# A retention and gated-MLP kernel: the planner's arrival time of program packets, and another order of loads and work

## The chip, the cores and the metric

The kernel runs on one core of a Trainium2 chip. The metric is the device time of one execution in microseconds, the median of the runs. It was 203.94 us before the change, over three runs from 202.18 to 205.26 us.

## The reference

Inputs are q, k, v of shape (4 batches, 8 heads, 768 tokens, 64), all float32, and the MLP's weights. A retention layer feeds a gated MLP:

```
state[b,h] = gamma[h] * state[b,h] + outer(k[t], v[t])
y[b,h,t]   = q[t] @ state[b,h] / 8
x    = y as (batch, 768, 512)
gate = sigmoid(causal depthwise convolution of x with conv_w, 5 taps)
out  = (gate * (x @ w_val)) @ w_out          # both weights 512 x 512
```

The output is (4, 768, 512) in float32.

## The kernel before

**Tiling.** The 768 tokens are cut into 6 chunks of 128, and a chunk of one batch is a "group" g (24 groups, chunk by chunk, the 4 batches within). Retention is done in chunks: scores of q and k, a mask, scores times v, and the state of earlier chunks times q. For the first four groups (chunk 0, batches 0 to 3) the steps stand apart: `first_scores` (called s below, L446 to L455), `first_mask` on VectorE, `first_y` (y, L523 to L532), `evac` (VectorE multiplies y by decay rows into the tile x, L588), `round_x` (ScalarE's cast xh) and `rest_x` (GpSimd's xl), and `first_state` (z, both halves of the state). The decay rows come from `first_pos` (p, a product of two matmuls with two rows each, L568) that `base_copy` moves out of PSUM. From group 4 on one `visit` (v) does the whole group in 128 small matmuls of 64x64, in two bursts. A `head` (h) opens them.

**The MLP.** x @ w_val is split in three products of rounded parts to keep float32 accuracy: `val_tile` (V, L1061; its matmuls in `val`, L719) has 12 matmuls of 512 columns per tile of 128 channels, 4 tiles per chunk. It ends in a gate (convolution on ScalarE and VectorE, a sigmoid) and a multiplication. The second product (O) is `out_tile` with 12 matmuls of 512 columns for chunks 0 and 5, and for chunks 1 to 4 seven block products of 12 matmuls of 256 columns. Weights arrive as 64-bit values and are converted on chip by ScalarE, VectorE and GpSimd (`convert`, w).

**Loads.** All input goes through SyncE's queue. The first 14 loads stand in `LOADS` (L61 to L64): ("a", g) is q, k and v of group g (768 KB), ("q", 0) is q and k of group 0 (512 KB), ("v", 0) its v (256 KB), ("k", g) the second layout of k that the state needs (256 KB), ("w", n) a weight row block (512 KB), and ("t", 0) the small table of decay and mask factors (68 KB). Later loads follow when a buffer is free.

**The order.** `WORK` (L66 to L70) is a string with one letter per PE step in the order of their due times. `plan` (L105 on) turns it into the instruction order of all engines on the host, ahead of time: a list scheduler that takes the step with the smallest rank among those ready, with a table of costs. The steps depend on each other by the tiles that they read and write. Where PE would wait early on, the planner puts filler matmuls on zeros into the order (L271 to L285); they are real instructions, and what follows them on PE follows in order.

**Program packets.** PE's program arrives by DMA in packets of 16 KB. The planner counts pairs (one weight load and one matmul): the first request is made after 71 pairs, each later one after 127.6 (L41). `fetch` sets when the packet that was asked for is usable. It looks at the loads that are in the list `sent` at that moment: the packet begins after the loads issued before the request, within limits, and is usable a little later. `offered` holds large loads back after 26 us of plan time, until PE is a set time past its last request.

In the planner of before, the time is worked out at the request, so a load that the planner takes up afterwards, though it starts earlier, is not in the list:

```
queued = max((x for t, x in sent if t <= asked + AHEAD), default=0.0)
later = min(max(asked + LEAD, queued + BEHIND), asked + WORST + 0.4 * (asked < 12.0)) + USABLE
```

Of the kernel before, what the change touches and what calls it, by code (L numbers as in the profile page):

```python
# [39 lines left out]
COLD, WARM_AT = 1.85, 5.0  # L40
FIRST_PAGE, PAGE = 71, 127.6  # L41
LEAD, AHEAD, BEHIND, WORST, USABLE, DEPTH = 1.0, 0.2, -0.9, 4.5, 2.4, 23
HOLD_FROM, HOLD, HOLD_LAG = 26.0, 30, 1.1
FIRST_BYTE, PER_MB = 2.85, 2.65
LATE_MB, LATE = 3.0, 1.2
TABLES = (4.6, 4.6)
# [12 lines left out]
FILLED_VALS = 24  # L59
CONV_LEAD, CHUNK = 7.0, 2.4  # L60
LOADS = (  # L61
    ("q", 0), ("t", 0), ("a", 1), ("v", 0), ("a", 2), ("w", 0), ("k", 1), ("a", 3),
    ("w", 1), ("w", 2), ("k", 0), ("w", 3), ("k", 2), ("k", 3),
)  # L64

WORK = (  # L66
    "spsysyzysyVzwzVwwhVzvVwvOOvOvOTvVvVvVVOvVOVv"
    "OVvvOvVOOOvVOOOOVVvOvVvVOVOVVOOOvvOOOvOvOOVO"
    "OOVOVVOOOOO"
)  # L70

# [33 lines left out]
def plan(steps, filler, last, into):  # L105
# [46 lines left out]
    left = [0] * len(steps)  # L152
# [8 lines left out]
    while ends:  # L161
        t = ends.pop()
# [8 lines left out]
    clock, free = {}, {}  # L171
# [8 lines left out]
        if not s.waits:  # L180
            offer(s)
    order, landed, moved = [], 0.0, 0.0
    left, need, usable, later = float(FIRST_PAGE), float(FIRST_PAGE + DEPTH), 0.0, 0.0
    kind, sent, asked_at = "big", [], -1e9

    def fetch(now):

        nonlocal left, need, usable, later, asked_at  # L190
        if left <= 1e-9:
            asked = max(now, usable)
            asked_at = asked
            queued = max((x for t, x in sent if t <= asked + AHEAD), default=0.0)
            later = min(max(asked + LEAD, queued + BEHIND), asked + WORST + 0.4 * (asked < 12.0)) + USABLE
            left = PAGE
        else:
            now = max(now, usable)
            usable, need = later, PAGE
        return now  # L200

    def run_pe(s, now):
        nonlocal left, need, kind
        slow = COLD if now < WARM_AT else 1.0
        if s.small:
            if kind == "big":
                now += INTO
            kind = "small"
            todo, each = s.small, PAIR * s.wide * slow
        else:  # L210
            if kind == "small":
                now += OUT_OF
            kind = "big"
            todo, each = s.big, s.gap / max(1, s.big) * slow
        while todo > min(left, need):
            x = min(left, need)
            now += x * each
            todo -= x
            left -= x
            need -= x  # L220
            now = fetch(now)
        left -= todo
        need -= todo
        now += todo * each
        return now, now + (0.21 if s.small else 0.17) * slow
# [9 lines left out]

    def offered(e):
        if e == "DMA" and patient and max(clock[e], clock["PE"]) > HOLD_FROM:
            if left <= HOLD or clock["PE"] < asked_at + HOLD_LAG:
                return [s for s in free[e] if s.mb < 0.4]
        return free[e] if e != "PE" or held is None else [s for s in free[e] if s is held]  # L240

# [18 lines left out]
    while any(free.values()):  # L260
        patient = True
        patient = any(offered(e) for e in free)
        start, _, e = min(
            (round(max(clock[e], min(max(s.ready, s.own if s.engine == e else 0.0) for s in offered(e))), 6), e, e)
            for e in free
            if offered(e)
        )
        s = min(
# [3 lines left out]
        if e == "PE":  # L272
# [5 lines left out]
            for i in range(int((start - since) * FILLED / FILL) if filling else 0):  # L278
# [4 lines left out]
                x = min(left, 2.0 if ring == into[0] else 4.0)  # L283
# [34 lines left out]
        if s.turn:  # L318

            t, e = s.turn, s.turn.engine  # L320
# [10 lines left out]
def tile_retention_gated_mlp(  # L331
# [930 lines left out]
    with tc.manual_schedule():  # L1262
        for step in plan(steps, filler, vals[FILLED_VALS], ("ye", "sc")):
            traced = nc.cur_bb.bb.instructions
            seen = len(traced)
            step.fn(*step.args)
            if step.engine == "PE":
                traced_as[step] = [i.name for i in traced[seen:] if i.engine == mybir.EngineType.PE]
            if step.behind:


                first, at = step.behind
                names = traced_as[first]
                tc.add_manual_dep(
                    traced[-1], names[min(int(at / PAIR) // 2 if first.small else 0, len(names) - 1)],
                    mybir.DependencyInfo(mybir.DependencyClass.Sync, mybir.DependencyReason.DATA), reason="load",
                )
# [93 lines left out]
```

## Time and profile before

| what | value |
|---|---|
| runs | 202.18, 203.94, 205.26 us |
| profiled execution | 205.48 us, its span 203.7 us |
| PE (matmul) busy | 196.7 us, 97% of the span |
| PEld (weight loads) | 168.5 us, 83% |
| VectorE / ScalarE / GpSimd | 130.3 / 110.2 / 140.4 us |
| DMA | 36.28 MB, mean 178 GB/s |
| chain that ended last | PE 86%, DMA 7%, VectorE 2% |

The profiled execution is 1.54 us above the median of the runs, and its span leaves 1.8 us outside. Matmuls are pipelined, so the ends of the records overlap the next ones; the starts tell more than the busy sum. In the rows below the times are microseconds from the span's start, and in brackets stands what ended an idle time.

### The profile page before, as it was taken

The numbers are of one execution on the slowest core, as the hardware profiler recorded it, in microseconds if no ns is written. First come the engines' busy times: TensorE is split into PE (matmuls) and PEld (weight loads), VectorE is DVE, ScalarE is ACT, GpSimd is POOL, SyncE is SP. The second block draws the span as 40 slices with busy tenths as digits, with TensorE's granted clock in tenths as the row PEclk, the third lists the DMA queues.
The fourth block names the chain that finished last, engine by engine and source line by source line (L and its number), as shares of the span: only waits on it lengthen the run. The fifth ranks groups of instructions, "written<-read, shape, count | busy, mean of one in ns | idle before, by whom it ended". The sixth has DMA issues, their size and how long they took to land.

```text
span 203.7 us, 8356 instructions
## 1 busy us (share of the span) xinstructions
PE 196.7 (97%) x3732; PEld 168.5 (83%) x3732; DVE 130.3 (64%) x200; ACT 110.2 (54%) x225; POOL 140.4 (69%) x120
## 2 busy tenths in 40 slices
PE   8899999999997999999999999999999999999993
PEld 5579876888885879899889899888889989888883
DVE  1355799862239986998489995998412558993100
ACT  3558867975177656965376566244433336612221
POOL 0049976899699986999949994766993799122500
PEclk9979999999999999999999999999999999999999
DMA  6999895578675640197657377311100122122022
GB/s 215 388 418 372 272 407 230 216 254 286 195 292 215 227 193 6 29 363 287 211 206 253 118 262 259 154 53 55 53 2 0 55 94 67 51 77 80 1 103 103
DMA packets 11303, 36.28 MB, mean 178 GB/s; under 512 B 1154, under 2 KB 5634, under 8 KB 8708
## 3 DMA queue, kind: packets, MB, share of 16 engines
q1 hardware_dynamic: 5472, 29.43, 39.2%
q10 hardware_dynamic: 5796, 6.32, 9.0%
q8 instruction: 29, 0.48, 0.9%
q14 instruction: 6, 0.05, 0.1%
HBM read 29.46 MB, written 6.29 MB: 176 GB/s over the span
## 4 chain that ended last, share of the span: by engine, by line
PE 86%; DMA 7%; DVE 2%; ACT 1%; issue 1%; SPq 0%; ACTq 0%
PE mm L726 33%; PE mm L803 20%; PE sy L511 10%; PE mm L846 8%; PE z_ps L495 5%; PE sy L433 4%; DMA out_dram<-o_sb 4%; DMA att<-in_att_dram 3%; PE sy L886 3%; PE ye L528 1%; DVE acc L710 1%; PE z_ps L451 1%; PE sy L451 1%; DVE u L483 0%; ACT o_sb L859 0%
## 5 line engine op out<-in xcount | busy, mean ns | idle before, releaser
L710 DVE SCALAR_TENSOR_TENSOR acc<-x,cw_sb,acc 128x512 f32<-128x512 f32 x96 | 68.2, 748 | 7.7 <-ACT acc L708 7.4
L606 POOL TENSOR_TENSOR xl<-x,xh 128x512 fp32r<-128x512 f32 x24 | 30.9, 1288 | 17.3 <-ACT xh L601 15.6
L788 POOL TENSOR_TENSOR gvl<-gate,gvh 128x512 fp32r<-128x512 f32 x24 | 30.9, 1296 | 9.2 <-ACT gvh L784 7.3
L726 PE MATMUL mm<-xl,wvh 128*128 128x512 f32 x96 | 31.0, 398 | 0.0
L726 PE MATMUL mm<-xh,wvh 128*128 128x512 f32 x96 | 30.9, 404 | 0.0
L422 POOL TENSOR_TENSOR att<-att,small_sb 128x512 f32<-128x512 f32 x24 | 25.1, 1046 | 7.6 <-DMA att<-in_att_dram 4.2
L726 PE MATMUL mm<-xh,wvl 128*128 128x512 f32 x96 | 27.7, 396 | 0.0
L741 DVE TENSOR_TENSOR gate<-mm,gate 128x512 f32<-128x512 f32 x24 | 16.5, 687 | 13.8 <-PE mm L726 12.7
L460 DVE TENSOR_TENSOR u<-sy,small_sb 128x512 f32<-128x512 f32 x20 | 13.7, 684 | 14.2 <-PE sy L433 14.2
L784 ACT CAST gvh<-gate 128x512 fp32r<-128x512 f32 x24 | 14.4, 618 | 15.1 <-DVE gate L741 11.9
L771 POOL TENSOR_TENSOR gate<-gate 128x512 f32<-128x512 f32 x16 | 20.7, 1297 | 1.8 <-DVE gate L741 1.5
L506 ACT COPY snap<-z_ps 128x256 f32<-128x256 f32 x40 | 13.8, 375 | 14.2 <-PE z_ps L495 13.1
L726 PEld LDWEIGHTS mm<-xh,wvl 128*128 128x128 f32 x96 | 17.9, 188 | 4.0
L726 PEld LDWEIGHTS mm<-xl,wvh 128*128 128x128 f32 x96 | 17.9, 188 | 3.9
L601 ACT CAST xh<-x 128x512 fp32r<-128x512 f32 x24 | 14.8, 617 | 10.6 <-DVE x L591 10.6
L718 ACT ACTIVATE gate<-acc 128x512 f32<-128x512 f32 x24 | 14.3, 600 | 11.5 <-DVE acc L710 6.0
L708 ACT ACTIVATE acc<-x,cw_sb 128x512 f32<-128x512 f32 x24 | 16.5, 692 | 7.4 <-DVE x L591 6.5
L752 POOL TENSOR_TENSOR gvl<-gate,gvh 128x512 fp32r<-128x512 f32 x8 | 10.3, 1289 | 14.4 <-ACT gvh L748 14.3
L726 PEld LDWEIGHTS mm<-xh,wvh 128*128 128x128 f32 x96 | 17.1, 188 | 3.3
L591 DVE TENSOR_TENSOR x<-sy,dec 128x512 f32<-128x512 f32 x20 | 13.6, 681 | 5.4 <-PE sy L433 4.6
L511 PEld LDWEIGHTS sy<-u,att 64*64 64x64 f32 x640 | 11.2, 134 | 6.6 <-issue 2.2
L511 PE MATMUL sy<-u,att 64*64 64x64 f32 x640 | 13.9, 224 | 1.5 <-DVE x L591 1.5
(79 smaller groups left out, 380.5 us busy)
## 6 DMA issues: line engine op xcount, KB each, us to landing
att<-in_att_dram SPq DMA_DIRECT2D x20, 1024.0 KB, 6.9
wst<-in_w_dram SPq DMA_DIRECT2D x8, 512.0 KB, 9.4
out_dram<-o_sb ACTq DMA_DIRECT2D x15, 256.0 KB, 3.2
att<-in_att_dram SPq DMA_DIRECT2D x3, 768.0 KB, 8.7
out_dram<-top ACTq DMA_DIRECT2D x8, 256.0 KB, 3.8
att<-in_att_dram SPq DMA_DIRECT2D x5, 256.0 KB, 8.7
att<-in_att_dram SPq DMA_DIRECT2D x1, 512.0 KB, 3.7
out_dram<-gate ACTq DMA_DIRECT2D x2, 128.0 KB, 1.7
```

Of the source, the lines that this page charges most:

```text
L422: nc.gpsimd.tensor_tensor(v, v, vd_sb[:, c, :].unsqueeze(2).broadcast_to([P, 8, HALF]), op=ALU.mult)
L511: nc.tensor.matmul(sy[cols, h, off:off + HALF], lhsT=lhsT, rhs=rhs, start=start, stop=True, skip_group_check=True,)
L601: nc.scalar.copy(xh[n][:, :, b], xs[n][:, :, b, HALO:])
L606: nc.gpsimd.tensor_tensor(xl[n][:, :, b], xs[n][:, :, b, HALO:], xh[n][:, :, b].bitcast(F32), op=ALU.subtract)
L708: nc.scalar.mul(acc, x[:, :, 0:P], cw_sb[:, m, 0:1])
L710: nc.vector.scalar_tensor_tensor(acc, x[:, :, k:k + P], cw_sb[:, m, k:k + 1], acc, op0=ALU.mult, op1=ALU.add,)
L726: nc.tensor.matmul(vps[n, m], lhsT=w[:, m, ct * P:(ct + 1) * P], rhs=xx[n][:, ct].rearrange("p b t -> p (b t)"), start=(i == 0), stop=(i = ...
L741: nc.vector.tensor_tensor(gv, vps.pop((n, m)), gv, op=ALU.mult)
L771: engine.tensor_tensor(block(n, k), block(n, a), block(n, b), op=getattr(ALU, op))
L788: engine.tensor_tensor(low, block(n, k), operands[n, k, 0].bitcast(F32), op=ALU.subtract)
L803: nc.tensor.matmul(banks[bank][:, tt * 256:(tt + 1) * 256], lhsT=g[:, ct, tt * P:(tt + 1) * P], rhs=weight(w, part % 2)[:, ct], start=(k i ...
L846: nc.tensor.matmul(ops[n, b, cs.start][:, 0:cs.stop - cs.start], lhsT=gg[:, b * P:(b + 1) * P], rhs=w[:, ct, cs], start=(i == 0), stop=(i ...
```

## The change

Three edits. The planner works out a packet's arrival at the next request, from all loads issued up to the request, with a fixed time for requests before 12 us of plan time, and a cap of 4.2 in place of 4.5 between 12 and 26 us. `LOADS` and `WORK` get another order: v of group 0 goes up to second place ahead of the table, group 3 goes ahead of all second layouts of k, and of those group 1's is last. In `WORK` p is the first letter, s comes earlier, z stands twice ahead of the first V, and four V and one O stand ahead of the first visit. The upper limit on the hold of large loads is 99 and larger than any distance between requests.

```diff
-HOLD_FROM, HOLD, HOLD_LAG = 26.0, 30, 1.1
+HOLD_FROM, HOLD, HOLD_LAG, HOLD_WINDOW = 26.0, 30, 1.1, 99.0
 LOADS = (
-    ("q", 0), ("t", 0), ("a", 1), ("v", 0), ("a", 2), ("w", 0), ("k", 1), ("a", 3),
-    ("w", 1), ("w", 2), ("k", 0), ("w", 3), ("k", 2), ("k", 3),
+    ("q", 0), ("v", 0), ("t", 0), ("a", 1), ("a", 2), ("w", 0), ("a", 3), ("w", 1),
+    ("k", 0), ("w", 2), ("w", 3), ("k", 3), ("k", 2), ("k", 1),
 )
 WORK = (
-    "spsysyzysyVzwzVwwhVzvVwvOOvOvOTvVvVvVVOvVOVv"
-    "OVvvOvVOOOvVOOOOVVvOvVvVOVOVVOOOvvOOOvOvOOVO"
+    "psyssyzsyyzwwVzwVhwzVVOvvvOOvOvVvVvVvVOVTvVO"
+    "vOVOvOVOOvOVOvvVOOOOVvOvVVOVOvOVVOOvvOOOvOVO"
     "OOVOVVOOOOO"
 )
+    def arrival():
+        if asked_at < 12.0:
+            return asked_at + 5.0 + USABLE
+        began = asked_at + LEAD
+        if asked_at < HOLD_FROM:
+            queued = max((x for t, x in sent if t <= asked_at + AHEAD), default=0.0)
+            return min(max(began, queued + BEHIND), asked_at + 4.2) + USABLE
+        for t, x in sorted(sent):
+            if t <= asked_at + AHEAD:
+                began = max(began, x + BEHIND)
+        return min(began, asked_at + WORST) + USABLE
     def fetch(now):
         if left <= 1e-9:
-            asked = max(now, usable)
-            asked_at = asked
-            queued = max((x for t, x in sent if t <= asked + AHEAD), default=0.0)
-            later = min(max(asked + LEAD, queued + BEHIND), asked + WORST + 0.4 * (asked < 12.0)) + USABLE
+            if asked_at > -1e8:
+                usable = arrival()
+            asked_at = max(now, usable)
             left = PAGE
         else:
             now = max(now, usable)
-            usable, need = later, PAGE
+            need = PAGE
     def offered(e):
-            if left <= HOLD or clock["PE"] < asked_at + HOLD_LAG:
+            if left <= HOLD or not 0 <= clock["PE"] - asked_at - HOLD_LAG <= HOLD_WINDOW:
```

## Rows read from the trace of the kernel before

**Rows 1.** Stages: stretch, length; busy us (instructions) by engine; clock, DMA share, GB/s
```profile
22.90:61.90 39.00, 39.00 (x866) 31.07 (x859) 24.68 (x38) 26.68 (x57) 32.76 (x29) 1.00 0.75 269
61.90:63.43 1.53, 0.02 (x1) 0.00 (x0) 1.53 (x4) 1.00 (x4) 1.53 (x2) 1.00 0.91 344
63.43:189.28 125.85, 125.71 (x2374) 111.46 (x2375) 94.16 (x144) 65.98 (x132) 94.70 (x79) 1.00 0.37 130
```

**Rows 2.** Waits of PE: who waited for whom; us in total, times, longest
```profile
PE sy L511 <- DVE x L591: 1.5, 1, 1.5
...
PE ye L879 <- PEq L1358: 0.8, 1, 0.8
```

**Rows 3.** Chain of waits, 48 to 64 us: start, us, what
```profile
48.80 8.18 DMA out_dram<-o_sb
...
57.06 0.18 ACT o_sb L859
...
62.78 0.61 DVE x L591
```

**Rows 4.** Timeline of PE, 5 to 23 us: start, us, engine, line, operation
```profile
5.46 1.26 PE L451 MATMUL sy<-att 64*64 64x128 f32 x32
...
6.65 1.12 PE L570 MATMUL ye<-u 2*128 2x512 f32 x2
...
8.73 0.90 PE L451 MATMUL z_ps<-att 64*64 64x128 f32 x32 [0.96 <-DMA att<-in_att_dram]
...
11.95 1.42 PE L451 MATMUL sy<-att 64*64 64x128 f32 x32
...
15.93 1.60 PE L886 MATMUL sy<-const-float32-0.0 128*128 128x128 f32 x12
...
17.47 0.90 PE L451 MATMUL z_ps<-att 64*64 64x128 f32 x32
...
20.28 1.60 PE L886 MATMUL sy<-const-float32-0.0 128*128 128x128 f32 x12
...
21.81 1.16 PE L495 MATMUL z_ps<-att 64*64 64x64 f32 x64
...
22.90 1.20 PE L726 MATMUL mm<-xh,wvh 128*128 128x512 f32 x4
```

**Rows 5.** Timeline of VectorE, ScalarE and GpSimd in the start
```profile
4.62 0.76 DVE L472 TENSOR_TENSOR xh<-small_sb 128x256 f32<-128x256 f32 x2 [3.69 <-DMA small_sb<-in_small_dram]
...
18.43 0.96 DVE L483 TENSOR_TENSOR u<-z_ps,xh 128x768 f32<-128x768 f32 x1 [1.67 <-PE z_ps L451]
...
19.43 1.05 POOL L422 TENSOR_TENSOR att<-att,small_sb 128x512 f32<-128x512 f32 x1
...
20.41 0.69 DVE L591 TENSOR_TENSOR x<-ye,base 128x512 f32<-128x512 f32 x1 [0.43 <-PE ye L528]
...
21.14 0.62 ACT L601 CAST xh<-x 128x512 fp32r<-128x512 f32 x1 [0.50 <-DVE x L591]
```

**Rows 6.** DMA issues at 2.5, 4.4 and 12.5 us; last column us to landing
```profile
att<-in_att_dram SPq DMA_DIRECT2D x1, 768.0 KB, 8.7
...
att<-in_att_dram SPq DMA_DIRECT2D x1, 768.0 KB, 10.7
...
att<-in_att_dram SPq DMA_DIRECT2D x1, 256.0 KB, 8.4
```

**Rows 7.** Stage with the reduced clock, columns as in Rows 1
```profile
9.80:13.00 3.20, 3.20 (x57) 2.86 (x55) 1.54 (x2) 2.06 (x6) 0.58 (x1) 0.50 1.04 423
```

**Rows 8.** Pairs up to two requests; DMA queues in 91.9:93 and 158.2:159.3
```profile
0.00:88.07 88.07, 84.40 (x1985) 68.87 (x1989) 57.51 (x89) 58.71 (x126) 66.03 (x60) 0.98 0.68 251
...
0.00:157.43 157.43, 153.76 (x3261) 130.43 (x3265) 107.78 (x166) 94.11 (x196) 121.37 (x105) 0.99 0.58 210
...
q8 instruction: 1, 0.02, 5.0%
...
q8 instruction: 1, 0.02, 7.7%
```

More of the change, by code (lines that the diff above doesn't have):

```diff
@@ L182, in plan @@
     order, landed, moved = [], 0.0, 0.0
-    left, need, usable, later = float(FIRST_PAGE), float(FIRST_PAGE + DEPTH), 0.0, 0.0
+    left, need, usable = float(FIRST_PAGE), float(FIRST_PAGE + DEPTH), 0.0
     kind, sent, asked_at = "big", [], -1e9
+    def arrival():
[9 more added lines that the diff above has]
+        return min(began, asked_at + WORST) + USABLE
     def fetch(now):
-        nonlocal left, need, usable, later, asked_at
+        nonlocal left, need, usable, asked_at
         if left <= 1e-9:
-            asked = max(now, usable)
-            asked_at = asked
-            queued = max((x for t, x in sent if t <= asked + AHEAD), default=0.0)
-            later = min(max(asked + LEAD, queued + BEHIND), asked + WORST + 0.4 * (asked < 12.0)) + USABLE
+            if asked_at > -1e8:
+                usable = arrival()
+            asked_at = max(now, usable)
             left = PAGE
```

## The prediction

> **What bounds the kernel now.** I read the stages first, then PE's waits, then the chain of waits where it leaves PE, then the timeline of the start. From 22.90 us, where the first V begins, PE's busy time fills its stages: 39.00 of 39.00 us, then 125.71 of 125.85 us. Between them lies one hole of 1.53 us [rows 1]. The list of PE's waits shows the same hole as a wait for an evacuation by VectorE, and besides it a wait of 0.8 us for PE's own sequencer at the very start [rows 2]. So after 22.90 us the time is the sum of PE's work, the hole and a tail, and the number of matmuls there does not change with the order. What an order can change is when V begins, what PE has already done by then, and the holes.
>
> The hole has its origin in a store: one output transfer issued at 48.80 us took 8.18 us, ScalarE's next copy into that buffer could only go on at 57.06 us, VectorE's taps came late behind it, and the evacuation for which PE waited began at 62.78 us [rows 3].
>
> The start is a chain through group 3. Its load was issued at about 4.4 us and landed 10.7 us later, at 15.1 us [rows 6]. Yet its scores began at 17.47 us: PE first did 12 filler matmuls, 15.93 us on, 1.60 us long [rows 4]. The planner had put them there to cover a wait that was over by then. After the scores come the mask at 18.43, the evacuation at 20.41 and the cast at 21.14, which ends at 21.76 us [rows 5]. PE fills 20.28 us on with another 12 fillers, and only at 21.81 us does it do the first two z, 64 small matmuls in 1.09 us up to V's start [rows 4].
>
> **The change part by part.**
>
> *Loads.* In the old list 3.82 MB end with group 3's load (0.5, 0.07, 0.75, 0.25, 0.75, 0.5, 0.25, 0.75 in its order), in the new one 3.57. Group 2's load, issued at 2.5 us, lands at 11.2 us, group 3's 1.5 MB of queue later at 15.1 us [rows 6], which is 2.6 us per MB. The 0.25 MB less are worth 0.65 us: group 3 lands at about 14.5 us. Group 1's load and the table come 0.25 MB later, 0.65 us. Group 1's scores now start at 8.73 us after an idle 0.96 us [rows 4], so they go to 9.4 us; group 2's load keeps its place, and the next scores after those start at 11.95 us [rows 4], so 1.5 us of slack take it. The mask factors, at 4.62 us and 0.76 us long [rows 5], go to about 6.0 us at their end; the first mask needs them after the scores at 5.46 us have ended, 6.7 us now and later with p in front. That costs nothing, and without this cover 0.65 us.
>
> *p first.* It takes 1.12 us and now comes after the first scores, which start at 5.46 us and take 1.26 us [rows 4]. With p first they start at 6.6 and end at 7.8 us. What hides it is the idle stretch up to 8.73 us and the later load of group 1; if that cover goes, it costs 1.12 us.
>
> *s before y, and z ahead of V.* The new string lets group 3's scores go ahead of the third y, since tile dependencies follow the string. The scores can begin at 14.5 us at best. At worst PE comes to them as late behind the load as now (17.47 less 15.1, 2.4 us), at 16.9 us. I take 15.4 us, nearer to the best: PE is one y ahead of where it was, and the second half of the fillers (0.8 us) may still stand there. From the scores' start to the end of the cast it is now 4.29 us [rows 4, 5]. In the new order VectorE does one more evacuation in this chain, 0.69 us [rows 5], ahead of the last y; most of it, 0.6 us, is added: 4.9 us. So V can begin at 20.3 us in place of 22.90, a gross 2.6 us. Of the two z that lie ahead of V now, the first can slip into the chain's gaps, where PE does 1.60 us of fillers now: its k moves up from 5.07 to 4.32 MB, and GpSimd's scaling takes 1.05 us [rows 5]. The second needs group 1's k, now last in the list. The last load lands at 12.5 + 8.4 = 20.9 us [rows 6] and, the bytes being the same, does so again; with 1.05 us of scaling it is 22 us. So this z follows inside the V's and is 0.55 us that PE no longer has behind it. Net 2.05 us. With 14.5 us it is 2.95 us, with 16.9 us 0.55 us. If group 3's scores stay at 17.47 us, the longer chain (0.6) and the covered z (0.55) cancel: zero, the lower bound. A loss from this part would need V's own weights to be late; w 0 keeps its 2.82 MB, and w 1 moves up by 0.25 MB.
>
> *The clock.* From 9.80 to 13.00 us PE was granted 0.50, its level of 1.2 GHz, after the idle 0.96 us and the scores at 8.73; the scores at 11.95 took 1.42 us there, those at 17.47, at full clock, 0.90 us [rows 4, 7]. If such a stretch falls on scores, y and z after 14.5 us, each loses some 0.5 us, three of them 1.5 us. In the sum I leave the clock as it is; this bound lies inside the range of the term above (2.05 less 1.5 is 0.55).
>
> *The planner's packets.* The code computes no time on the chip; it only moves loads and fillers. No wait for a packet stands among PE's waits after the first [rows 2], so there is no such stall to remove: zero, and the nearest price for one that is made is the 0.8 us of that wait. That packets do wait for loads the trace shows twice. The planner's request falls on pair 1985 at 88.07 us, in a stretch with large loads, and the packet moved in 91.9 to 93 us, 3.8 us or more later; the one at pair 3261, 157.43 us, with only stores about, moved after 158.2 us, within 1.9 us [rows 8]. The Trainium skill, "DMA: Bandwidth & Descriptors", section "Queues, rings and completion order", says that each DMA engine goes round robin between the queue rows that have work, a packet at a time. By that rule a program packet would not stand behind loads issued earlier, the new waits would be plan fiction, and the sum would hold nothing for the planner's edit but misplaced fillers, as in the first rival. The two requests speak against it.
>
> *The later order.* Four V and one O stand ahead of the first visit, and visits come in other places. PE's work is the same: zero, as long as VectorE, ScalarE and GpSimd deliver. In the stage after 63.43 us they are busy for 94.16, 65.98 and 94.70 of 125.85 us [rows 1]. The last 11 letters are the same, so the tail is too. The hole of 1.53 us comes from a store among loads, and the new order puts the first stores elsewhere; it may go. Late next would be the evacuation that the following visit waits for.
>
> **The sum.** The profiled execution took 205.48 us. Less 2.05 us for the start and 1.53 us for the hole it is 201.9 us. It lies 1.54 us above the median of 203.94 us, just the hole's size, so I take it that the median run had none of it: 203.94 less 2.05 is 201.9 us as well.
>
> **The rivals.** *First, the start gains nothing:* fillers again stand in front of group 3's scores, because the planner's idea of the landing is wrong in the new order too. For it speaks that the fillers of 15.93 us were such an error; against it that the scores are now ahead of y and the packet's wait is set anew. The time stays at 203.9 us. *Second, all goes:* the scores start with the landing, 2.95 us, and the hole is a part of the median run as well and disappears. Then it is 203.94 − 2.95 − 1.53 = 199.5 us. Against it speaks that the fastest run before, 202.18 us, can hardly have had the hole, and then the median need not. *Third, slower:* the visits are bunched, and each waits for the evacuation of the one before. One such wait costs 1.5 us [rows 2]. It is in the stretch of "Ovvv" behind the first O and of the next "vv": with a start that gains nothing, three of them give 203.94 + 4.5 = 208.4 us; from two on, which outweigh the 2.05 us of the start, the kernel is slower than before. Against it speaks that the planner puts ready V and O between visits, and that visits made only one hole so far.
>
> **How the numbers follow.** The forecast has a chance of 0.50, with a range of its own from 201.0 (2.95 us) to 203.4 us (0.55 us). The first rival has 0.24, the second 0.17, the third 0.09. The likeliest gives 201.9 us. The range goes from 199.4 us, the second rival, to 205.0 us, the first with the spread of the runs (up to 1.3 us above the median), and leaves out the third and little else. Two per cent, about what a measurement of this kernel can tell, is 4.1 us: faster means under 199.9, slower over 208.0 us. Faster is the second rival with a hundredth of the first case, 0.18; slower the third from three waits on, 0.08; within it is the rest, 0.74.
>
> **What would show it.** In the changed kernel's timeline: p ahead of the first scores and no later start of the group 1 scores than 9.4 us; group 3's scores between 14.5 and 16.9 us, with fewer than 12 fillers ahead; one z ahead of the first V and one between V's; V's start near 20.3 us. In the stages: PE as full as now behind that, and no hole at the first stores. The prediction is wrong if V begins at 22 us or later, if the distance from V's start to the end grows by more than the one z, or if PE's waits show evacuations or its program several times.

## The result and the profile after

| | before | after |
|---|---|---|
| median (runs) | 203.81 us (202.18 to 205.26, 10 runs) | 205.87 us (205.14 to 207.68, 10 runs) |
| ratio | | 1.0122, interval 1.0088 to 1.0156 |
| profiled execution, its span | 205.48 us, 203.7 us | 205.27 us, 203.5 us |

The change made the kernel 1.2% slower; 201.9 us was forecast, with 205.0 us as the upper end of the range. The two profiled executions are nearly equal, so their difference is not what the median lost. Executions of the kernel before come with and without a stretch of reduced clock in the start, and the one profiled before had it; that has to be kept in mind in all that follows.

All lines of the code lie 9 further down in the changed kernel (V's matmuls at L735, the scores of a visit at L442).

The stages first, in the columns of [rows 1]: from V's start to the hole, the hole, from there to the last product, the stretch of [rows 7], and the pairs up to one request.

```profile
20.94:115.90 94.96, 94.96 (x2240) 79.79 (x2241) 74.51 (x115) 63.38 (x133) 83.89 (x72) 1.00 0.65 228
115.90:117.94 2.04, 0.23 (x16) 0.09 (x5) 0.00 (x0) 1.28 (x4) 2.04 (x3) 1.00 0.18 59
117.94:189.21 71.27, 71.11 (x1025) 62.81 (x1026) 46.41 (x71) 29.74 (x56) 44.95 (x37) 1.00 0.25 87
9.80:13.00 3.20, 1.80 (x46) 1.40 (x50) 1.78 (x3) 1.18 (x2) 1.27 (x1) 1.00 1.01 416
0.00:108.98 108.98, 106.07 (x2495) 87.80 (x2496) 76.81 (x119) 71.70 (x154) 84.17 (x75) 1.00 0.71 254
```

The hole of 62 us [rows 1] is gone and PE is full as before, but for a new hole of 2.04 us at 116 us. And the clock is 1.00 where it was 0.50 [rows 7]. PE's waits, to be held against [rows 2], name what ended the hole:

```profile
PE sy L442 <- issue: 1.8, 1, 1.8
PE sy L460 <- DMA att<-in_att_dram: 1.5, 1, 1.5
PE ye L888 <- PEq L1367: 0.8, 1, 0.8
PE mm L735 <- ACT xh L610: 0.4, 1, 0.4
```

"issue" means that PE waited for no semaphore that the profile shows. PE's timeline there:

```profile
115.56 0.57 PE L442 MATMUL sy<-att 64*64 64x64 f32 x25
117.94 0.34 PE L442 MATMUL sy<-att 64*64 64x64 f32 x7 [1.81 <-issue]
```

It stops in the middle of the 32 scores of a visit, between matmuls that depend on nothing new. What stops there is the program. SyncE's timeline has one load near it, and the DMA queues of 109:115.6 us (first two lines) and 115.6:116.75 us (third) show what moved:

```profile
111.21 0.33 SPq L418 DMA_DIRECT2D att<-in_att_dram  x1
```

```profile
q1 hardware_dynamic: 139, 1.04, 41.6%
q10 hardware_dynamic: 64, 0.06, 2.7%
...
q8 instruction: 1, 0.02, 5.5%
```

By the planner's count the packet was asked for at 108.98 us (pair 2495 in the stages). It did not move before 115.6 us, 6.6 us later; until then the queues hold the load of group 20, 1 MB, issued 2.2 us after that request. The two requests of [rows 8] had waited about 1 and 4 us.

The start, to be held against [rows 4]:

```profile
4.92 1.12 PE L579 MATMUL ye<-u 2*128 2x512 f32 x2
5.97 0.90 PE L460 MATMUL sy<-att 64*64 64x128 f32 x32
...
8.88 0.85 PE L460 MATMUL z_ps<-att 64*64 64x128 f32 x32
...
11.20 0.90 PE L460 MATMUL sy<-att 64*64 64x128 f32 x32 [1.48 <-DMA att<-in_att_dram]
...
13.49 2.05 PE L895 MATMUL sy<-const-float32-0.0 128*128 128x128 f32 x16
15.47 0.90 PE L460 MATMUL z_ps<-att 64*64 64x128 f32 x32
...
18.77 0.65 PE L504 MATMUL z_ps<-att 64*64 64x64 f32 x32
...
20.94 1.20 PE L735 MATMUL mm<-xh,wvh 128*128 128x512 f32 x4 [0.43 <-ACT xh L610]
...
23.70 0.52 PE L504 MATMUL z_ps<-att 64*64 64x64 f32 x20
```

p is ahead of the first scores, group 3's scores start at 15.47 us (15.4 us was forecast), one z lies ahead of V and the next behind it, and V starts at 20.94 us instead of 22.90. The steps of the start came out, but for one sign: fewer than 12 fillers were to stand ahead of group 3's scores, and 16 do. So there are two questions: what the hole costs the median, and why a start that looks 1.96 us better does not help.

### The profile page after: what moved, and what is told of

It is laid out like the page before. It is cut to its first block, busy times and chain, and to the rows that moved or that the text cites. A ratio compares the mean times of both kernels' runs of the same rounds, so it can differ in the third digit from the quotient of the medians.

```text
span 203.5 us, 8347 instructions
## 1 busy us (share of the span) xinstructions
PE 195.5 (96%) x3730; PEld 166.1 (82%) x3730; DVE 130.7 (64%) x200; ACT 109.8 (54%) x225; POOL 140.0 (69%) x120
## 4 chain that ended last, share of the span: by engine, by line
PE 90%; DMA 4%; issue 1%; ACT 1%; SPq 1%; DVE 1%; ACTq 0%
PE mm L735 34%; PE mm L812 20%; PE mm L855 12%; PE sy L520 11%; PE z_ps L504 5%; PE sy L442 5%; DMA att<-in_att_dram 4%; PE sy L895 1%; SPq L418 1%; ACT xh L610 1%; DVE u L492 0%; PE sy L460 0%; PE z_ps L460 0%; PE ye L537 0%; ACT up L646 0%
## 5 line engine op out<-in xcount | busy, mean ns | idle before, releaser
L719 DVE SCALAR_TENSOR_TENSOR acc<-x,cw_sb,acc 128x512 f32<-128x512 f32 x96 | 67.0, 749 | 3.5 <-ACT acc L717 3.1
L735 PE MATMUL mm<-xl,wvh 128*128 128x512 f32 x96 | 31.2, 400 | 0.0
L735 PE MATMUL mm<-xh,wvh 128*128 128x512 f32 x96 | 30.2, 405 | 0.5 <-ACT xh L610 0.4
L735 PE MATMUL mm<-xh,wvl 128*128 128x512 f32 x96 | 28.3, 395 | 0.0
L735 PEld LDWEIGHTS mm<-xh,wvl 128*128 128x128 f32 x96 | 17.8, 188 | 3.7
L735 PEld LDWEIGHTS mm<-xl,wvh 128*128 128x128 f32 x96 | 17.9, 188 | 3.6
L735 PEld LDWEIGHTS mm<-xh,wvh 128*128 128x128 f32 x96 | 17.0, 188 | 4.0 <-ACT xh L610 0.6
L812 PE MATMUL mm<-wst,gvh 128*128 128x256 f32 x96 | 16.6, 285 | 0.0
```

The source lines that it names most:

```text
L719: nc.vector.scalar_tensor_tensor(acc, x[:, :, k:k + P], cw_sb[:, m, k:k + 1], acc, op0=ALU.mult, op1=ALU.add,)
L735: nc.tensor.matmul(vps[n, m], lhsT=w[:, m, ct * P:(ct + 1) * P], rhs=xx[n][:, ct].rearrange("p b t -> p (b t)"), start=(i == 0), stop=(i = ...
L812: nc.tensor.matmul(banks[bank][:, tt * 256:(tt + 1) * 256], lhsT=g[:, ct, tt * P:(tt + 1) * P], rhs=weight(w, part % 2)[:, ct], start=(k i ...
```

## The experiments

Before any of them, one answer comes from the programs themselves. The old planner given the new LOADS and WORK emits the program of after, instruction for instruction with its waits. (The new planner given the old lists emits the instructions of before in their order, but three waits of SyncE for PE stand elsewhere.) So all of the difference between the two kernels is the order of loads and work.

Theory A: the new order issues group 20's load just ahead of a program request, the packet waits for the whole load, and this is the loss behind V. Theory K: the start's gain was measured against an execution with the clock at 0.50; at full clock the old order is as early. Rival B: the loss lies in the new order of visits, and the hole is a trait of single executions. Theory D, named in some of the expectations: what the new start gains is paid back behind V.

### The hole

**after_again** is the changed kernel once more, **before_again** the old one.

> The changed kernel once more, unaltered, for a second trace. Theory A (a program packet behind a load): PE stands still again inside the visit near 116 us, waiting for nothing the trace names (its program), for some 2.0 us, and the packet moves only after the load issued near 111 us. Theory B (chance: a store or a load came late in the one profiled execution): the hole near 116 us is gone or elsewhere.

> The kernel before once more, unaltered, for a second trace. If the hole of 1.5 us near 62 us belongs to the slow executions only, it is absent here or the time is near 205 us; without it the time is 203.0 to 204.0 us and the last matmul comes 1.7 us earlier than in the first trace. If it stands in every execution, it is here at a time near 203.8 us too.

The changed kernel took 206.24 us with the same hole at the same place, 2.2 us of wait for "issue". The old one took 204.71 us with no hole behind V, so the hole of 62 us in [rows 3] belonged to that execution, and the new one belongs to the program. V started at 23.34 us, with the clock at 0.55 in the stretch of [rows 7]; more of that below.

**load20_later, load20_1us_later, load20_1us_earlier** shift the time to which the planner ties group 20's load.

```diff
-                to = asked_at + HOLD_LAG - 0.3
+                to = asked_at + HOLD_LAG - 0.3 + (2.5 if s.args[0] == 20 else 0.0)
```

(+1.0 and −1.3 in the other two.)

> The changed kernel; only the load of group 20 (issued near 111 us) is tied to a PE instruction 2.5 us later; every engine's order stays. Theory A: the program packet is asked for before the load and moves near 111 to 113 us, the 2.0 us hole near 116 us goes, the time falls from 205.9 to about 203.9 us (as before the change or just below). Theory B: the hole was chance, the median stays at 205.9 us. Theory C (the later order costs on its own): stays above 205 us.

> The changed kernel; the load of group 20 is tied to a PE instruction 1.0 us later than in the changed kernel (2.5 us in the run before), all orders as they are. Theory A, the packet loses to a load that is issued shortly ahead of it: if the chip's request comes within 1 us of the load, the hole is gone as with 2.5 us; if it comes later, the hole stays and grows by about 1 us, to 3.0 to 3.4 us, since the load ends 1 us later. Theory B (a set delay of the packet that has nothing to do with the load): 2.0 to 2.4 us as it was.

> The changed kernel; the load of group 20 is tied to a PE instruction 1.3 us earlier, all orders as they are. Theory A: the packet still stands behind the load, which is over 1.3 us earlier, so the hole shrinks from 2.0 to 2.4 us to 0.7 to 1.1 us. Theory B: 2.0 to 2.4 us as it was.

The tie reaches no further than the last PE step already planned, so the load moved less than meant: +1.0 and +2.5 emit one and the same program. So load20_1us_later did not test what its expectation set against each other. after_load20_narrow, below, has the same tie. What counts is where the load came relative to pair 2495, and how long the pause in the scores was beyond the usual 0.34 us:

| kernel | load issued behind pair 2495 | hole | profiled execution |
|---|---|---|---|
| load20_1us_earlier | 0.95 us | 0.9 us | 204.40 us |
| after | 2.23 us | 2.0 us | 205.27 us |
| after_again | 2.22 us | 2.4 us | 206.24 us |
| load20_later | 2.46 us | 0 | 203.75 us |
| load20_1us_later, the same program | 2.46 us | 0.5 us | 204.46 us |
| after_load20_narrow, the same tie | 2.46 us | 1.3 us | 205.19 us |

(Four traces, load20_moved's among them, lack the record of one matmul at 2.8 us; the pairs are counted with it.) PE's waits of load20_1us_earlier, load20_1us_later and after_load20_narrow; load20_later has no such wait:

```profile
PE sy L442 <- issue: 0.6, 1, 0.6
```

```profile
PE sy L442 <- issue: 0.2, 1, 0.2
```

```profile
PE sy L442 <- issue: 1.1, 1, 1.1
```

Up to 2.23 us, the earlier the load, the shorter the hole: the packet waits for the end of a load that is already under way. At 2.46 us it is chance: by the DMA queues the packet moved after 0.1, 0.4 and 0.7 MB of the load, in the order of the last three rows, and the hole grew with it. That is theory A. It also puts the chip's request near the moment when this load's data begin to move, some 2 to 3 us after the planner's count, here where PE runs long matmuls and pairs are rare; this is an estimate. load20_later's median, 204.61 us, ratio 1.0066 (1.0033 to 1.0099), does not size the hole, since its program has it in one of two profiled executions.

**load20_moved** takes the load away from the request altogether.

```diff
+        late = next(s for s in order if s.fn is load and s.args[0] == 20)
+        i = order.index(late)
...
+        j, first = next((j, s) for j, s in ahead if s.start > late.start + 2.2)
+        order.insert(j, order.pop(i))
+        late.behind = (first, 0.0)
```

> The changed kernel with one edit: the load of group 20 is really taken up later in the order, behind the first PE step that the plan starts more than 2.2 us after it, so that the load is issued safely behind PE's request (load20_later had moved it by 0.2 us only). Theory A (the packet's wait is the loss behind V): no hole in the visit near 116 us in the profile, load issued 3 us or more behind pair 2495, and the median falls from 205.9 to 203.7 to 204.2 us. Rival B (the loss is elsewhere and the hole only a trait of the profiled execution): the median stays above 205 us. Theory K (at full clock the new start is worth nothing): the median stays above 202.9 us even so, because one z is still to be done behind V.

203.60 us (202.89 to 205.60, 12 runs), ratio to before 0.998 (0.9948 to 1.0013). The load goes out at 114.60 us (SyncE's timeline), and the packet moves alone in 112:114.5 us (queues), so PE goes through the visit without a pause (PE's timeline):

```profile
114.60 0.33 SPq L418 DMA_DIRECT2D att<-in_att_dram  x1
```

```profile
q8 instruction: 1, 0.02, 3.5%
```

```profile
116.14 0.65 PE L442 MATMUL sy<-att 64*64 64x64 f32 x32
116.72 1.21 PE L812 MATMUL mm<-wst,gvh 128*128 128x256 f32 x8
```

One load issued 2.8 us later against pair 2495 (5.03 us behind it, not 2.23), and nothing else changed in the program, takes 2.27 us off the median (205.87 to 203.60). The two medians come from different series; against the kernel before in each, the ratio falls from 1.0122 to 0.998, with intervals far apart. Rival B expected more than 205 us. The hole is the loss.

### The start and the clock

**before_filled** keeps the old order and puts 4 matmuls of 512 columns behind p, in place of 4 of the 72 short warm-up matmuls, so that the number of pairs stays. **before_third** is the kernel before, in the same series.

```diff
+        for i in range(4):
+            warm_up(1)
...
-        for i in range(SHORT):
+        for i in range(SHORT - 4):
```

> The kernel before, with 4 of the 72 short warm-up matmuls replaced by 4 of 512 columns right behind p, in the idle stretch ahead of group 1's scores; nothing else moves. Theory K: the clock stays full in the start in most executions, the first V begins near 21.5 us, the median falls from 203.9 to about 202.9 us. Rival L: the median stays at 203.9 us.

> The kernel before, a third trace. Theory K (the clock decides the old start): if the granted clock of this execution is 1.00 all through the start, group 3's scores begin near 16.0 us and the first V near 21.5 us, and the time is 202.3 to 203.6 us; with a stretch at 0.50 they are again near 17.5 and 23 us, and the time is 203.8 to 205 us. Rival L (the landing decides): 17.5 and 23 us whatever the clock.

First before_third, the stretch of [rows 7] (the clock is the third column from the right) and V in PE's timeline, then the same two views of before_filled:

```profile
9.80:13.00 3.20, 3.20 (x68) 2.96 (x66) 1.65 (x2) 0.79 (x3) 0.00 (x0) 0.59 1.04 421
```

```profile
23.12 1.20 PE L726 MATMUL mm<-xh,wvh 128*128 128x512 f32 x4
```

```profile
9.80:13.00 3.20, 2.79 (x97) 2.46 (x90) 2.54 (x4) 3.20 (x10) 0.88 (x1) 1.00 1.04 421
```

```profile
18.66 1.60 PE L888 MATMUL sy<-const-float32-0.0 128*128 128x128 f32 x12
20.19 1.16 PE L495 MATMUL z_ps<-att 64*64 64x64 f32 x64
21.28 1.19 PE L728 MATMUL mm<-xh,wvh 128*128 128x512 f32 x4
```

At 2.4 GHz throughout, the old order starts V at 21.28 us with both z done. The seven profiles of after and of its kernels with group 20's load shifted had V at 20.94 us in after and at 21.35 to 21.69 us in the others, with one z still to do. So theory K holds as far as these profiles go: at the same clock the new start gains nothing. (It is not the clock alone: in filled_narrow, below, the old order had full clock and V at 22.81 us, because group 2's scores waited 1.37 us for their load. Landings vary.) The runs say the same. Of the 25 runs of the kernel before that stand beside load20_moved, 9 had a mean granted clock of 0.997 or more and a median of 202.75 us, and 16 less than that, and 204.06 us (203.98 us without the four above 205 us). The new order without the hole, always at full clock in that series, had 203.60 us, 0.85 us above the old one at full clock. before_filled itself measured 202.99 us, ratio 0.9981 (0.9951 to 1.0012): by its ratio alone the fall that K forecast is not clear of noise.

Behind V the new order is longer too. Both at full clock, load20_moved and before_filled took 203.72 and 202.25 us in their profiled executions, 1.47 us apart. The lines show V, the z behind it and the last product of load20_moved, then the last product of before_filled:

```profile
21.54 1.21 PE L735 MATMUL mm<-xh,wvh 128*128 128x512 f32 x4 [0.43 <-ACT xh L610]
...
24.30 0.69 PE L504 MATMUL z_ps<-att 64*64 64x64 f32 x32
24.93 0.50 PE L735 MATMUL mm<-xh,wvh 128*128 128x512 f32 x1
25.27 0.39 PE L735 MATMUL mm<-xl,wvh 128*128 128x512 f32 x1
25.50 0.40 PE L735 MATMUL mm<-xh,wvh 128*128 128x512 f32 x1
...
198.51 0.27 PE L855 MATMUL mm<-woh,gvl 128*128 128x256 f32 x1
```

```profile
197.03 0.27 PE L848 MATMUL mm<-woh,gvl 128*128 128x256 f32 x1
```

V starts 0.26 us later (21.54 and 21.28 us), and from there to the last product it is 176.97 us in place of 175.75, 1.22 us more without any hole. The z between V's matmuls holds PE for 0.63 us, and the first V matmul behind it 0.34 us where the next takes 0.23; the prediction had 0.55 us for it. The other half microsecond is open.

**new_start_old_rest, loads_alone, work_alone** split the order: the changed kernel with the old letters behind the first "VV"; the old kernel with the new LOADS; the old kernel with the new WORK.

```diff
-    "psyssyzsyyzwwVzwVhwzVVOvvvOOvOvVvVvVvVOVTvVO"
-    "vOVOvOVOOvOVOvvVOOOOVvOvVVOVOvOVVOOvvOOOvOVO"
+    "psyssyzsyyzwwVzwVhwzVVvvOOvOvOTvVvVvVVOvVOVv"
+    "OVvvOvVOOOvVOOOOVVvOvVvVOVOVVOOOvvOOOvOvOOVO"
```

> The changed kernel with the new list of loads and the new string up to the first O, and behind that the letters in the order of the kernel before. Theory A: the start's gain of 1.4 us (V 1.96 us earlier, one z more behind it) shows if no load comes between a request and its packet: 202.4 us; with one such hole 204.4 us. Theory C: the later part of the new string is what costs, so 202.0 to 203.0 us here. Theory D (the new start itself is paid back behind, by ScalarE and VectorE work that it pushes on): 204 us or more without a wait for the program.

> The kernel before with the new list of loads alone. Theory A+K (a program packet behind a load makes 2.0 to 2.4 us of the loss, one z more behind V 0.55 us, and the start gains next to nothing against old executions at full clock): no new wait for the program, 203 to 204.5 us. Theory D (the new start pushes work back that is paid later): a loss of over 1 us here.

> The kernel before with the new string of work alone, the old list of loads. Theory A+K: the loss sits in the later letters, where a load falls between a request for program and its packet; if it falls there again, a hole of about 2 us within a visit and 205 to 206.5 us; if the plan puts that load elsewhere, 203 to 204.5 us. Theory D: 204 us or less, since the new start needs the new loads.

new_start_old_rest: 204.05 us, ratio 1.0002 (0.9965 to 1.0039), no wait for the program behind V. The new start with the old rest is no gain, and the old rest has no hole. A's figure for this run, 202.4 us, still counted the start's gain and was missed; D's, 204 us or more without a wait for the program, was met. K says why the gain is none, and the 1.22 us above say that a part is paid back behind V, as D has it. D's reason, work of ScalarE and VectorE pushed on, is not shown: no such wait of PE stands behind V here. loads_alone: 206.67 us over 4 runs, ratio 1.0148 (1.009 to 1.0207), and here I had expected no wait for a packet. PE's waits:

```profile
PE sy L511 <- DVE x L591: 1.3, 1, 1.3
PE mm L846 <- issue: 1.1, 1, 1.1
PE sy L433 <- issue: 0.8, 1, 0.8
```

Its V starts earliest of all, at 20.68 us, and it is the slowest kernel: two waits for the program and one for an evacuation fall among the first visits, at 42 to 63 us. That a load which moves anywhere shifts which requests it meets is the reading that fits; no run moved these loads. work_alone: 205.14 us, ratio 1.0086 (1.0045 to 1.0127), without such a wait, where 203 to 204.5 us had been expected for that case; this loss is not explained. Its profiled execution, 207.03 us, is one of three of its ten above 206.9 us, and its start shows something else; a stretch, then p and V in PE's timeline:

```profile
5.00:13.00 8.00, 8.00 (x92) 5.09 (x94) 1.73 (x4) 3.15 (x11) 0.00 (x0) 1.00 1.01 396
```

```profile
5.46 2.07 PE L570 MATMUL ye<-u 2*128 2x512 f32 x2
...
23.51 0.50 PE L726 MATMUL mm<-xh,wvh 128*128 128x512 f32 x1
```

p takes 2.07 us where it takes 1.12 us else, as at 1.2 GHz, though the clock column says 1.00. The profile of new_start_old_rest (205.14 us, one of four of its ten above 205 us) has the same p and V at 23.11 us. Why some executions begin so is open.

### The fillers

What stands ahead of the two z in before_filled are 12 fillers of 1.60 us. Four kernels go at the fillers.

> The kernel before with the idle stretch behind p filled, as in the run before, and the last 12 fillers, ahead of the first two z, cut from 128 to 32 columns. The z then begin when GpSimd has scaled their k, near 19.1 us in place of 20.19 us, and V near 20.2 us in place of 21.28 us: median 202.0 us, 1 us under the filled kernel (202.99). If V waits for something else (w 0, the cast of x), 203.0 us.

> The changed kernel with the load of group 20 2.5 us later, and the 16 fillers ahead of group 3's scores cut from 128 to 32 columns. My first rival's mechanism: those fillers still stand between the landing near 14.3 us and the scores at 15.5 to 16.1 us. Without them the scores begin near 14.5 to 15 us, V near 20 us, and the median falls by about 1 us, from 204.6 to 203.6 us. If the landing binds, V stays at 21 to 21.5 us and the median at 204.6 us.

> before_filled (old order, clock kept up by four 512 column matmuls) with its last 12 filler matmuls, which stand ahead of the two z and took 1.60 us, on 32x32 weights in place of 128x128. If a filler's price is its weight load, they shrink to 0.8 us or less, z starts near 19.4 us and V near 20.3 us in place of 21.28 us, and the median goes from 203.0 to about 202.1 us. If it is a fixed price per instruction, they stay at 1.5 us and the time at 203.0 us. If the clock falls because PE does less, a stretch at 0.50 shows in the first V's and the time rises by 1 us or more.

> As filled_short, and also the 12 and 8 fillers around the scores of group 3 (1.60 and 1.16 us) on 32x32 weights. The scores of group 3 start when their load lands, 15.0 to 15.4 us in place of 15.85; V starts near 19.9 us and the median is about 201.7 us. If the clock falls in the start as in before's disturbed executions, V starts after 21.5 us and the time is 203.5 us or more.

filled_narrow and after_load20_narrow cut the moving columns of a filler from 128 to 32 (`dst[:, 0:min(cols, dst.shape[1])]`, cols = 32), the second with load20_later's edit besides. filled_short also cuts the weights to 32 columns (`zero.broadcast_to([P, 32])`, so 128x32 and not the 32x32 of the expectation) in the last 12 fillers, filled_all_short in the last 32. The 12 fillers of filled_narrow, then of filled_short with what follows them:

```profile
20.26 1.52 PE L893 MATMUL sy<-const-float32-0.0 128*128 128x32 f32 x12
```

```profile
18.87 0.56 PE L895 MATMUL sy<-const-float32-0.0 128*32 128x32 f32 x12
19.98 1.16 PE L496 MATMUL z_ps<-att 64*64 64x64 f32 x64 [0.54 <-POOL att L423]
21.07 1.20 PE L729 MATMUL mm<-xh,wvh 128*128 128x512 f32 x4
```

A quarter of the columns leaves 1.52 of 1.60 us; a quarter of the weight columns leaves 0.56 us. The Trainium skill says as much in "TensorE: Matmul & The Clock Gate", section "LDWEIGHTS (loading the stationary operand)": a weight load is paid by its columns. So filled_narrow (202.95 us, 0.9997, 0.9956 to 1.0038) tested nothing of what it was for. after_load20_narrow (205.34 us over 4 runs, 1.0119, 1.0052 to 1.0186) had as little of it: its 16 fillers still took 1.97 us. So what the fillers ahead of group 3's scores cost the new start was not measured.

filled_short: 202.39 us, ratio 0.9951 (0.9921 to 0.9982). filled_all_short: 202.11 us, ratio 0.9921 (0.9885 to 0.9956). Both are faster than either kernel, by 0.5 and 0.8%, with no new order at all. Their V came only 0.2 us earlier than before_filled's (21.07 and 21.15 us), not 1 us and more as I had expected: the z behind the fillers now waits for GpSimd's scaling of its k, 0.54 us in the row above. How the gain divides between the clock, the fillers and the chip of that series is not settled; the interval of filled_short overlaps that of before_filled.

## Why the prediction was wrong

1. **"The planner's packets: zero."** This step failed and made the sign. It took the list of waits of before, which held no stall for the program, as a statement on the new order, and priced one that is made at 0.8 us. The order made one of 2.0 to 2.4 us, and without it the median is 2.27 us lower. Only the text of the planner was costed; that a move of visits and V shifts every pair count, and with it which load stands in front of which request, was not. [rows 8] held the price: the packet among loads moved 3.8 us or more after its request, and in that place it was not missed.
2. **"The later order: zero, as long as VectorE, ScalarE and GpSimd deliver."** They did. PE's program is one more supplier, and it was left out of the condition. The hole lies in this part of the order: new_start_old_rest, without it, is 1.8 us faster than after.
3. **"Net 2.05 us" for the start.** This step failed too. The events came within 0.7 us of their forecast, and V moved by 1.96 us in that profile. But it was subtracted from an execution whose PE ran at 1.2 GHz for 3.2 us [rows 7]. At 2.4 GHz the old order has V at 21.28 us with both z done, and the term is zero or a little less. "I leave the clock as it is" was the error: the median of before is a mixture, and the new order (p and its fillers ahead) mostly runs at full clock. Of the 2.05 us at most some 0.3 us reached the median (203.90 to 203.60 without the hole), and that is not clear of noise. Of the 0.85 us that it stays above the old order at full clock, one z explains 0.6 to 0.7 us as a z between V's matmuls costs; the rest is open. The prediction's own sign for this, a distance from V's start to the end that grows by more than one z, came true: without the hole it grew by 1.22 us between the two profiles at full clock.
4. **"I take it that the median run had none of it",** of the hole of 62 us. This fits: it is in neither repeat of the kernel before.
5. **The rivals.** The slower one named bunched visits that wait for evacuations; no such wait is in after's list. The first, a start that gains nothing, came true in its outcome. Its own reason, fillers in front of group 3's scores, is not what the runs showed; they showed the clock in its place. But it is not excluded as a part: 2.05 us of them stand there still, the scores started when they were forecast with them, and the kernel that was to shorten them did not.
6. **Packets and queues.** The prediction set the round robin of the Trainium skill, "DMA: Bandwidth & Descriptors", section "Queues, rings and completion order", against the two requests of [rows 8], and trusted the requests. The runs bear that out: here a packet waits for a megabyte issued ahead of it. That does not show the round robin wrong: no run shows in what portions an engine takes the load's share. The Trainium skill, "Runtime: NRT & Kernel Launch", section "Instruction fetch mechanics", holds that the fetch is hidden because instructions issue more slowly than they are filled in. In most of the trace it is hidden. At 116 us it is not, by 2.0 us.

The sum as measured: 203.81 us before; the packet +2.27; start, clock and all else the remaining −0.2, not clear of noise; 205.87 us after.

## What to carry to other kernels

When an order of work changes, count the program's own fetches as transfers that can be late: look for each request, ask which large load stands in front of it and how soon PE needs the packet, and keep such a load behind the request by more than the count is uncertain (2 to 3 us here). Before a gain at the start is subtracted, look at the granted clock of the profiled execution there and at the spread of the runs; if the old kernel also runs at the higher level, measure it there. Where fillers only keep a wait covered, give them few weight columns.

## What the runs showed of the hardware

- A program packet of 16 KB, asked for with a load of 1 MB ahead of it, moved only behind that load's data: 6.6 us after the counted request; by the same count eight of the other eleven packets from 97 us on began 0.7 to 1.7 us after theirs. With the load gone it still took 3.6 us from the counted request, which puts the real request some 2 to 3 us later than the count, an estimate. With the load issued 2.46 us behind the count the packet could move in the middle of it, after 0.1, 0.4 or 0.7 MB.
- Twelve fillers took 1.60 us on 128x128 weights with 128 columns, 1.52 us with 32 columns, and 0.56 us on 32 weight columns.
- Four matmuls of 512 columns in the idle stretch after p held the clock at 1.00 in the start's profile, where the kernel before had 0.50 to 0.59 in all three of its profiles, after an idle stretch ahead of group 1's scores.
- At a granted clock of 1.00 an execution can still begin with matmuls at half speed (p 2.07 instead of 1.12 us) until about 13 us.
